# Agent attention followed by a softmax feed-forward layer: p split ahead of its turn, row factors through DRAM, k first in the head, five u buffers, and a new planned order

## The chip, the cores and the metric

The kernel runs on one core of a Trainium2 chip. The metric is the device time of one launch in microseconds (us). Three runs of the kernel before gave a median of 1497.92 us (1496.82 to 1499.42).

## The reference

Four batches, 12608 tokens each, 128 channels, 49 agents, 1024 hidden columns, all in float32:

```python
def sm(a, b):
    s = scale * (a @ b.transpose(0, 2, 1)); s = s - s.max(-1, keepdims=True)
    e = np.exp(s); return e / (e.sum(-1, keepdims=True) + 1e-09)
agent_v = sm(agents, k) @ v
x = sm(q, agents) @ agent_v                      # [50432, 128]
h = x @ w_in                                     # [50432, 1024]
e = np.exp(h - h.max(-1)); solu = h * e / (e.sum(-1) + 1e-09)
ln = (solu - mean) / sqrt(var + 1e-06) * g_ln
out = ln @ w_out
```

## The kernel before, in words

**Tiles and engines.** Tokens are cut into 396 tiles of 128 (99 a batch), and two tiles make a pair. As `agent_v @ w_in` is the same for all tokens of a batch, it is made once a batch (phase A: scores of k, maximum, exponential, transposes, product with v, then `f1` to `f4l`, lines 570 to 590) and kept in two parts, `mh` and `ml`, whose sum is the full value; each has two buffers (`mpool`). Phase B makes the softmax p of 8 tiles of q over the agents: products (line 694), maximum, exponential, sum, then per group of 4 tiles a scaled `pack` on GpSimd (POOL, 722), two transposes on TensorE (PE, 729), a copy to SBUF on ScalarE (ACT, 737), a split into high and low part on POOL (743, 748), and four transfers on SyncE's queue (SP, 767) that place both parts in `pT`, the high one and the low one in different halves of the partitions.

**Each tile x** then goes through `c_h` (824: h in PSUM, four instructions on PE, `pT` against `mh` and `ml`), `c_max` (828, VectorE, DVE), `c_exp` (838, ACT), `c_u` (843, DVE: u = h times e, two buffers of u), and `c_sq` (849, ACT: the sum of squares). Half of the pairs are of kind Z: u is turned on PE (856), copied to SBUF on ACT (907), split into `uH` and `uL` on POOL (916, 920) and multiplied with w_out's two parts in 24 instructions a pair (937). The others are of kind Y: u is turned in 32x32 blocks on DVE (863), regrouped by 16 transfers a unit on SP's queue (871), and multiplied in full float32 (877). Two pairs of one kind make a unit of 4 tiles, with one output transfer (1025).

**The row factor** (one over the standard deviation) is made on POOL in eight small steps (951 to 972). For a Z unit it is turned on DVE (976), sent to DRAM (980), and read back by all partitions as `rB` (984); `c_fin` (1020, DVE) multiplies PSUM by `rB` into `ob`, which is sent out. For a Y unit POOL makes a 128x128 tile `dy` (1002), PE multiplies it with `quad` (1007), and ACT or DVE copies the 128x4 result to `yp` (1011), by which `c_fy` (885 on ACT, 887 on DVE) multiplies.

**The order** is fixed ahead by `Plan.run`: each operation has an engine, a cost, a due time (`D...` constants, in tiles) and what it depends on; the plan always issues next what can start first, and among what can start at about the same time (`EPS`) the one due first. All instructions of an engine then run in that order, and SP's transfers too, each behind the one before it. Transfers are all issued by SP. `WC` = 4 is the number of Z products that are planned as one operation, `YC` = 2 that of Y products (a Y product is two instructions in the profile). Four PSUM banks (`px`) serve everything but h; h has two buffers of two banks. In the head (batch 0), loads of k and v alternate, each product with v following its scores; free times on PE before the first tile are filled with small products (1035).

Of the kernel before, what the change touches and what calls it, by code (L numbers as in the profile page):

```python
# [19 lines left out]
class Op:  # L20


    __slots__ = ("eng", "fn", "cost", "due", "left", "outs", "deps", "take", "free", "bank", "start", "end", "by", "ready", "kind", "shy")


class Plan:
# [8 lines left out]
    SWITCH = ((0.0, 0.0, 0.09), (0.0, 0.0, 0.09), (0.15, 0.12, 0.0))  # L35

    HOLD = 0.12

    def __init__(self, banks):
# [4 lines left out]
        self.kind = 0  # L44

# [14 lines left out]
    def push(self, o):  # L60
        o.ready = {}
        for e in o.eng:
            o.ready[e] = max([0.0] + [d.end + (self.LAT.get(d.by + e, 0.2) if d.by != "S" else 0.0) for d in o.deps])
            self.cand[e].append(o)

    def run(self, idle=None):
        while True:
            best = None
            for e, ops in self.cand.items():
                if not ops:  # L70
                    continue
                free = [b[0] for b in self.banks if b[0] is not None]
                first = min(free) if free else None
                at, opts, low = self.at[e], [], None
                for o in ops:
                    s = max(at, o.ready[e])
                    if o.take:
                        if first is None:
                            continue
                        s = max(s, first)  # L80
                    opts.append((s, o))
                    low = s if low is None else min(low, s)
                if low is None:
                    continue
                near = [z for z in opts if z[0] <= low + self.EPS[e]]
                if e == "P" and self.kind == 2:
                    near = [z for z in opts if z[0] <= low + self.HOLD and z[1].kind == 2] or near
                s, o = min(near, key=lambda z: z[1].due)
                if o.shy > 0.0:
                    s, o = min((z for z in opts if z[0] <= s + o.shy), key=lambda z: z[1].due)  # L90
                if best is None or s < best[0]:
                    best = (s, e, o)
            if best is None:
                break
            s, e, o = best
            for z in o.eng:
                self.cand[z].remove(o)
            if o.take:
# [5 lines left out]
            o.start, o.by = s, e  # L104
            if e == "S":
                hold, size, lag = o.cost
                self.at[e] = s + hold
# [43 lines left out]
def kernel(  # L151
# [25 lines left out]
    CPR = 5.63  # L177
    UTB = 3
# [7 lines left out]
    WC = 4  # L186

    BD0 = 5.03
    BD1 = 15.85
    BD2 = 1.88  # L190
    BD3 = -20.87
    BD4 = -3.24
    BD5 = 3.07
    DH = -9.08
    DMX = 6.59
    DEX = 1.64
    DU_ = -21.8
    DSQ = 15.3
    DT = -0.97
    DEV = 13.79  # L200
    DLD = 12.64
    DSP = 16.84
    DW = 13.2
    DR = 15.79
    DF_ = 37.93
    OUTD = 20.02
    OUTC = -69.6
    VA = 3
    VA1 = 12
    QA = 22.03  # L210
    WA = -7.03
    VLAG = 0.74
    PTB = 4
    SHY = 0.31
    DHR = 5.82
    DHL = -9.02
    DMXR = 19.87
    DMXL = 0.06
    DEXR = -2.43
    DEXL = -3.57  # L220
    DUR = -30.17
    DUL = 17.14
    DSQR = -54.86
    DSQL = 4.96
    DTR = -20.36
    DTL = -14.12
    DEVR = -17.55
    DEVL = 7.51
    DLDR = -20.48
    DLDL = -18.62  # L230
    DSPR = -1.34
    DSPL = -11.65
    DWR = -2.28
    DWL = 3.97
    RBL = 2.38
    ASP = 0.86
    MZ = 5.66
    B7G = True
    B7 = 7.35
    DTB = 4.24  # L240
    DMV = -0.75
    DMS = 0.0
    MVC = 2
    DWY = 11.65
    DWS = 4.05
    YC = 2
    DFY = 5.09
    DTBR = -5.14
    DTBL = -8.26
    ASTART = -4.09  # L250
    AEND = 0.95
# [8 lines left out]
    mpool = ctx.enter_context(tc.tile_pool(name="mpool", bufs=2))  # L260
# [11 lines left out]
    make_identity(nc, ident)  # L272
    ones = const.tile([P, P], F32, name="ones")
# [13 lines left out]
    def pair_f64(dst, names):  # L287
# [5 lines left out]
        def tmp():  # L293
            for k, tg in (("s", "e"), ("a", "e"), ("e", "u"), ("m", "u")):
                t = epool.tile([P, 2, HW], I32, tag=tg, bufs=2, name=f"c{k}_{names}")
                for h in range(2):
                    z[k, h] = t[:, h, :]
# [37 lines left out]
    def load_out():  # L335
        nc.sync.dma_start(out=g_sb, in_=g_ln)
        for h in range(2):
            wd = words["out", h] = mpool.tile([P, HW, 2], I32, tag="mh" if h == 0 else "ml", name=f"wd_out{h}")
# [6 lines left out]
    def conv_out():  # L345
# [8 lines left out]
        def sums(q):  # L354

            n = NF >> (q + 1)
            if q == 0:
                pm["s"] = epool.tile([P, NF // 2, C], F32, tag="sq", bufs=1, name="ws")
# [32 lines left out]
    for i in range(2):  # L391
        pk = const.tile([P, GT, AP2], F32, name=f"pack{i}")
        nc.gpsimd.memset(pk, 0.0)
        packs.append(pk)
# [9 lines left out]
    fold32 = const.tile([P, SQB], F32, name="fold32")  # L404
    nc.vector.tensor_reduce(out=fold32, in_=ident.rearrange("p (a c) -> p c a", c=SQB), op=ALU.add, axis=AX.X)
    quad = const.tile([P, GT], F32, name="quad")
    nc.vector.tensor_reduce(out=quad, in_=ident.rearrange("p (a c) -> p a c", c=SQB), op=ALU.add, axis=AX.X)
    ph2 = [ps_h.tile([P, DF], F32, name=f"ph{i}") for i in range(2)]
    plan = Plan([ps_x.tile([P, HW], F32, name=f"px{i}") for i in range(4)])
    op = plan.op  # L410
# [9 lines left out]
    def phase_a(b, due, gate):  # L420
# [14 lines left out]
        def kload(c):  # L435
            w = CT * P if c < NCK else CKT
            if not head:
                kts[c] = kpool.tile([C, CT * P], F32, tag="kt", name=f"kt{b}_{c}")
            else:
                if c % 4 == 0:  # L440
                    kts["t"] = ypool.tile([C, 4, CT * P], F32, tag="tb", name=f"kh{b}_{c}")
# [3 lines left out]
        def vload(c):  # L445
            if head:
                if c % 4 == 0:
                    vts["t"] = ypool.tile([P, 4, CT, C], F32, tag="uY", name=f"vh{b}_{c}")
# [51 lines left out]
        def p2_et(c, k="D"):  # L500
            px = ps.pop(("t", c))
            w = HW if c < NCK else TX
            eT = res["eT", c] = bpool.tile([P, HW], F32, tag="eT", name=f"eT{b}_{c}")
# [100 lines left out]
        def kop(c):  # L604
            if c < NC and c not in K:
                old = M1.get(c - 1) if not head else M1.get(c - 5 - c % 4)
                K[c] = op("S", st(kload, c), (0.45, sz(c), 0), -199 + 0.2 * c if head else at(c * 2.55 - 3), gate + [old])

        def vop(c):
            old = M2.get(c - 1) if not head else M2.get(c - 5 - c % 4)  # L610
# [4 lines left out]
        FC = {}  # L615
        for c in range(NC):
# [9 lines left out]
            if c:  # L626
                FC[c] = op("A", st(p1_fc, c), 0.2, at(z + 0.6), [N1[c], AC.get(c - 4)])
            TT[c] = op("P", st(p2_t, c), 0.435 * fr(c), at(z + 1), [EE[c], M2.get(c - 2)], take=True)
            ET[c] = (op("A", st(p2_et, c, "A"), 0.478 * fr(c), at(z + 1.2), [TT[c]], free=TT[c]) if head and c < HEADA else
                     op(ETE, st(p2_et, c), (0.478 * fr(c), 0.6 * fr(c)), at(z + 1.2), [TT[c]], free=TT[c]))  # L630
            vop(c)
            M2[c] = op("P", st(p2_mm, c), 0.88 if c < NCK else 0.42, at(z + MZ) if not head else at(z + 1.5),
                       [ET[c], V[c], M2.get(c - 1), AC.get(c - 2)], take=True, kind=2)
            AC[c] = op("D", st(p2_ev, c), 0.26, at(z + 1.8), [M2[c], FC.get(c), AC.get(c - 1)], free=M2[c])
# [46 lines left out]
    def phase_b(k, dues, gate=()):  # L681
# [36 lines left out]

        def b4(q):
            m = min(GT, nt - q * GT)  # L720
            sl = slice(q * GT, q * GT + m)
            nc.gpsimd.tensor_tensor(out=packs[q][:, :m, :A], in0=r["d"][:, sl, :],
                                    in1=r["s"][:, sl].unsqueeze(2).to_broadcast([P, m, A]), op=ALU.mult)

        def b5(q, px):
            m = min(GT, nt - q * GT)
            r["pt", q] = px
            for j in range(0, m, 2):
                nc.tensor.transpose(px[:, j * AP2 : (j + 2) * AP2], packs[q][:, j : j + 2, :].rearrange("p j a -> p (j a)"),
                                    ident)  # L730

        def b6(q):
            w = (min(GT, nt - q * GT) + 1) // 2 * P
            r["n", q] = bpool.tile([P, 2, GT // 2 * P], F32R, tag="pn", bufs=2, name=f"pn{b}_{t0}_{q}")
            if B7G:
                r["f", q] = bpool.tile([P, GT // 2 * P], F32, tag="pf", bufs=2, name=f"pf{b}_{t0}_{q}")
                nc.scalar.copy(out=r["f", q][:, :w], in_=r.pop(("pt", q))[:, :w])
            else:
                nc.scalar.copy(out=r["n", q][:, 0, :w], in_=r["pt", q][:, :w])

        def b7h(q):
            w = (min(GT, nt - q * GT) + 1) // 2 * P
            nc.gpsimd.tensor_scalar(out=r["n", q][:, 0, :w], in0=r["f", q][:, :w], scalar1=1.0, scalar2=0.0, op0=ALU.mult, op1=ALU.add)

        def b7l(q):
            w = (min(GT, nt - q * GT) + 1) // 2 * P
            pn = r["n", q]
# [496 lines left out]
```

## Time and profile before

| | before |
|---|---|
| median of three runs | 1497.92 us |
| profiled execution | 1496.0 us, of which the span 1494.2 us |
| busy PE / DVE / ACT / POOL | 1447.1 / 1371.5 / 1291.3 / 1110.3 us |
| transfers issued on SP's queue, largest groups | uY x768, pT x392 |
| mean granted clock of PE | 0.995 of full |

Busy times are those of instructions on an engine; PE's ends are modelled, and its instructions overlap, so its busy time counts short pauses as work. The chain is the work that ended last, followed back: a piece "1.44 PE px L937 x12" says that twelve instructions of line 937 took 1.44 us of the path. An idle time names what ended it.

### The profile page before, as it was taken

How to read it: one execution, taken by the hardware profiler on the slowest of the kernel's cores; microseconds unless marked ns; L12 is line 12 of the kernel's file. 1: busy time of each engine (PE TensorE's matmuls, PEld its weight loads, DVE VectorE, ACT ScalarE, POOL GpSimd, SP SyncE). 2: the span in 40 equal slices, each digit the busy share in tenths (PEclk: the TensorE clock that was granted, in tenths of full speed). 3: DMA queues.
4: the chain of work that ended last, by engine and by line, in shares of the span. 5: the costliest groups of instructions: out<-in, count | busy, mean ns of one | idle time of the engine just before them, and what ended most of it. 6: DMA issues, size and time to landing. Idle time of an engine off the chain costs nothing.

```text
span 1494.2 us, 34108 instructions
## 1 busy us (share of the span) xinstructions
PE 1447.1 (97%) x11954; PEld 1285.0 (86%) x11954; DVE 1371.5 (92%) x1987; ACT 1291.3 (86%) x2536; POOL 1110.3 (74%) x1569
## 2 busy tenths in 40 slices
PE   8889999999999999999999999899999999999999
PEld 5668889898988989989887888789889898989998
DVE  7799999999999999999998898699999999999996
ACT  4688989889988988899887898688899999999995
POOL 2667787788778777787786677677788888888875
PEclk9999999999999999999999999999999999999999
DMA  9565676676577668756657655567546656566461
GB/s 371 163 179 156 177 186 160 174 184 153 144 194 202 165 179 215 181 137 158 155 140 200 184 156 157 147 175 206 138 118 157 152 126 166 137 154 162 114 155 57
DMA packets 142698, 247.72 MB, mean 166 GB/s; under 512 B 26048, under 2 KB 80320, under 8 KB 142528
## 3 DMA queue, kind: packets, MB, share of 16 engines
q1 hardware_dynamic: 142528, 245.54, 63.1%
q8 instruction: 96, 1.57, 0.5%
q14 instruction: 74, 0.61, 0.1%
HBM read 92.77 MB, written 26.05 MB: 80 GB/s over the span
## 4 chain that ended last, share of the span: by engine, by line
PE 56%; ACT 13%; DVE 10%; DMA 10%; issue 5%; SPq 4%; POOL 2%; DVEq 0%; ACTq 0%; POOLq 0%
PE ph L824 15%; PE px L877 14%; PE px L937 11%; PE px L856 6%; ACT e L838 5%; DVE u L843 4%; DMA rB<-dr 4%; ACT sq L849 4%; DVE nm L828 3%; PE px L465 3%; SPq L871 3%; PE px L514 3%; DMA dr<-yr 2%; ACT uT L907 2%; PE px L694 2%
## 5 line engine op out<-in xcount | busy, mean ns | idle before, releaser
L849 ACT ACTIVATE sq<-u,su 128x1024 bf16<-128x1024 f32 x396 | 460.7, 1163 | 53.4 <-DVE u L843 49.2
L843 DVE SCALAR_TENSOR_TENSOR u<-ph,e 128x1024 f32<-128x1024 f32 x396 | 474.6, 1217 | 29.4 <-ACT e L838 13.6
L838 ACT ACTIVATE e<-ph,nm 128x1024 f32<-128x1024 f32 x396 | 442.8, 1124 | 60.6 <-DVE nm L828 58.9
L828 DVE TENSOR_REDUCE nm<-ph 128x1 f32<-128x1024 f32 x396 | 467.8, 1206 | 28.2 <-PE ph L824 26.8
L920 POOL TENSOR_TENSOR uL<-uT,uH 128x1024 fp32r<-128x1024 f32 (+1 forms) x198 | 470.7, 2377 | 14.5
L877 PE MATMUL px<-w,uY 128*128 128x128 f32 x3072 | 383.0, 276 | 1.7 <-ACT uT L907 1.0
L877 PEld LDWEIGHTS px<-w,uY 128*128 128x128 f32 x3072 | 365.9, 192 | 8.7 <-ACT uT L907 2.3
L824 PE MATMUL ph<-mh,pT 128*128 128x512 f32 x792 | 336.5, 425 | 8.6 <-DVE u L843 5.4
L824 PE MATMUL ph<-ml,pT 128*128 128x512 f32 x792 | 312.8, 395 | 0.0
L916 POOL TENSOR_SCALAR uH<-uT 128x1024 fp32r<-128x1024 f32 (+1 forms) x198 | 207.6, 1048 | 99.2 <-ACT uT L907 99.0
L937 PE MATMUL px<-uH,wH 128*128 128x256 f32 x816 | 238.7, 292 | 0.6 <-POOL x L957 0.3
L863 DVE STREAM_TRANSPOSE tb<-u 128x1024 f32<-128x1024 f32 x192 | 237.2, 1238 | 1.3
L937 PE MATMUL px<-uL,wH 128*128 128x256 f32 x816 | 235.7, 289 | 0.0
L907 ACT COPY uT<-px 128x512 f32<-128x512 f32 x394 | 220.8, 595 | 16.7 <-PE px L856 12.9
L937 PE MATMUL px<-uH,wL 128*128 128x256 f32 x816 | 235.0, 288 | 0.0
L856 PE MATMUL px<-ident,u 128*128 128x128 f32 x1632 | 223.0, 274 | 6.8 <-DVE ob L1020 4.0
L856 PEld LDWEIGHTS px<-ident,u 128*128 128x128 f32 x1632 | 191.2, 141 | 33.4 <-DVE ob L1020 5.1
L824 PEld LDWEIGHTS ph<-mh,pT 128*128 128x128 f32 x792 | 149.8, 189 | 43.7 <-DVE u L843 13.5
L824 PEld LDWEIGHTS ph<-ml,pT 128*128 128x128 f32 x792 | 150.1, 189 | 19.5 <-DVE ml L590 0.3
L937 PEld LDWEIGHTS px<-uH,wL 128*128 128x128 f32 x816 | 153.8, 189 | 5.0 <-issue 2.3
L937 PEld LDWEIGHTS px<-uH,wH 128*128 128x128 f32 x816 | 153.9, 189 | 4.8 <-issue 1.3
L937 PEld LDWEIGHTS px<-uL,wH 128*128 128x128 f32 x816 | 154.1, 189 | 4.2 <-issue 1.1
(132 smaller groups left out, 1595.9 us busy)
## 6 DMA issues: line engine op xcount, KB each, us to landing
uY<-tb SPq DMA_DIRECT2D x768, 128.0 KB, 2.9
pT<-pn SPq DMA_DIRECT2D x392, 64.0 KB, 2.2
qt<-in_qT_dram SPq DMA_DIRECT2D x48, 512.0 KB, 4.4
kt<-in_kT_dram SPq DMA_DIRECT2D x36, 512.0 KB, 4.4
vt<-in_v_dram SPq DMA_DIRECT2D x36, 512.0 KB, 4.8
rB<-dr SPq DMA_DIRECT2D x50, 256.0 KB, 3.7
out_dram<-ob SPq DMA_DIRECT2D x50, 256.0 KB, 2.6
out_dram<-oy SPq DMA_DIRECT2D x48, 256.0 KB, 2.8
```

The source lines that it names most:

```text
L824: nc.tensor.matmul(ph[:, sl], lhs, bmats[b]["mh" if m == 0 else "ml"][:, sl], start=(m == 0), stop=(m == 1))
L828: nc.vector.tensor_reduce(out=nms[x], in_=phs[x], op=ALU.max, axis=AX.X, negate=True)
L838: nc.scalar.activation(out=es[x], in_=phs[x], func=AF.Exp, bias=nms.pop(x), accum_out=st[G]["S"][:, j : j + 1])
L843: nc.vector.scalar_tensor_tensor(out=u, in0=phs[x], scalar=INV, in1=es[x], op0=ALU.mult, op1=ALU.mult, accum_out=su)
L849: nc.scalar.activation(out=sq, in_=u, func=AF.Square, bias=su, scale=-float(DF), accum_out=st[G]["Q"][:, j : j + 1])
L856: nc.tensor.transpose(pt[:, kf * P : (kf + 1) * P], us[x][0][:, k0 * P : (k0 + 1) * P], ident)
L863: nc.vector.transpose(to, us[x][0].rearrange("p (k r c) -> p k r c", r=GT, c=SQB))
L877: nc.tensor.matmul(st[G]["po"][:, a * P : (a + 1) * P], yb[G][1][:, a, kf].rearrange("p x c -> p (x c)"), w2[:, kf, :], start=(kf == 0), s ...
L907: nc.scalar.copy(out=rr[x][:, hf * 4 : hf * 4 + 4, :], in_=pt)
L916: nc.gpsimd.tensor_scalar(out=uH, in0=rr[x][:, k0:k1, :], scalar1=1.0, scalar2=0.0, op0=ALU.mult, op1=ALU.add)
L920: nc.gpsimd.tensor_tensor(out=uL, in0=rr[x][:, k0:k1, :], in1=uH.bitcast(F32), op=ALU.subtract)
L937: nc.tensor.matmul(po, wt[:, kf, :], ut[:, kf, :], start=(q == 0), stop=(q == WM - 1))
```

## The change

- **p is split before it is turned.** POOL scales p in place, rounds it to the high part and subtracts, into a `pack` of 4 x (64 high + 64 low) columns. One transpose a tile in F32R then gives `pT` with both parts in place; ACT copies it from PSUM (128x512) straight into `pT`. The copy to `pf`, the split behind it and the four transfers a group are gone.
- **The Y factor goes through DRAM**, as Z's does: turned on DVE, sent, and read back as 128x4 (`senty`); `y0`, `y1`, `y2` are gone.
- **Head:** all k is asked for first, then v; products with v come behind the whole of the scores, and `eT` of all chunks is kept (in the buffers of `uH`, `uL`). w_in and the first q are asked for behind v.
- **Buffers:** five of u in place of two, `UTB` 4 for 3, `sq` is written over e, `c_fin` writes over `rB` (three buffers), and in return `mh` and `ml` have one buffer: `f4h` waits for the last h of the batch before.
- **Order:** `WC` 12, `YC` 8 (8 products, 16 instructions); tiles' h in order; regrouping, factor and `rB` transfers may be issued by ACT too, but by the plan only where SP is some 30 us late with them, and one behind a long activation; the plan's costs of a change of kind on PE, and all due times, are other numbers.
- The last unit is sent in pieces of 256 bytes (four a partition and half) where it was 1 KB.

```diff
     mpool = ctx.enter_context(tc.tile_pool(name="mpool", bufs=2))
+    mpool = ctx.enter_context(tc.tile_pool(name="mpool", bufs=1))
...
-            o9 = op("A", st(f4h, hf), 0.571, at(z + 0.8 + 0.4 * hf), [o8, l0, last_h.get(b - 2)] + mdone[b])
+            o9 = op("A", st(f4h, hf), 0.571, at(z + 0.8 + 0.4 * hf), [o8, l0, last_h.get(b - 1)] + mdone[b])
...
         def b4(q):
+            nc.gpsimd.tensor_tensor(out=d, in0=d, in1=rs..., op=ALU.mult)
+        def b4h(q):
+            nc.gpsimd.tensor_scalar(out=packs[q][:, :m, 0, :A], in0=d, scalar1=1.0, scalar2=0.0, op0=ALU.mult, op1=ALU.add)
+        def b4l(q):
+            nc.gpsimd.tensor_tensor(out=packs[q][:, :m, 1, :A], in0=d, in1=packs[q][:, :m, 0, :A].bitcast(F32), op=ALU.subtract)
         def b5(q, px):
-            for j in range(0, m, 2):
-                nc.tensor.transpose(px[:, j * AP2 : (j + 2) * AP2], packs[q][:, j : j + 2, :]..., ident)
+            for j in range(m):
+                nc.tensor.transpose(px[:, j * P : (j + 1) * P].bitcast(F32R), packs[q][:, j]..., identR)
         def b6(q):
-            nc.scalar.copy(out=r["f", q][:, :w], in_=r.pop(("pt", q))[:, :w])
+            nc.scalar.copy(out=pt[:, : m * P], in_=r.pop(("pt", q))[:, : m * P])
...
-        us[x] = (epool.tile([P, DF], F32, tag="u", bufs=2, ...), ...)
+        us[x] = (epool.tile([P, DF], F32, tag="u", bufs=UBF, ...), ...)          # UBF = 5
-        sq = epool.tile([P, DF], BF16, tag="sq", bufs=1, name=f"sq{x}")
+        sq = es.pop(x).bitcast(BF16)[:, :DF]
...
-        EX[x] = op("A", F(c_exp, x), 1.11, at(x, DEX, DEXR, DEXL), [MX[x], U.get(x - 2), R2.get(G - SB + 1)] + (cout if x < 2 else []))
+        EX[x] = op("A", F(c_exp, x), 1.11, at(x, DEX, DEXR, DEXL), [MX[x], U.get(x - 2), SQ.get(x - 2), R2.get(G - SB + 1)] + (cout if x < 2 else []))
-        U[x] = op("D", F(c_u, x), 1.21, at(x, DU_, DUR, DUL), [EX[x], T.get((x - 2, 0)), T.get((x - 2, 1)), TBT.get(x - 2), SQ.get(x - 2)])
+        U[x] = op("D", F(c_u, x), 1.21, at(x, DU_, DUR, DUL), [EX[x], T.get((x - UBF, 0)), T.get((x - UBF, 1)), TBT.get(x - UBF), SQ.get(x - UBF)])
...
-                o = op("G", y0, 0.5, x + DR, [o, YP.get(back(G, 2))])
-                p = op("P", y1, 0.3, x + DR, [o], take=True)
-                YP[G] = op("AD", y2, (0.2, 0.08), x + DR, [p, FY.get(back(G, 3))], free=p)
+                TN[G] = op("D", turn, 0.12, x + DR, [o])
+                RB[G] = op("SA", send, (0.5, 0.01, 0), x + DR, [TN[G]])
+                YP[G] = op("SA", senty, (0.5, 0.15, 0), x + DRB, [RB[G], FY.get(back(G, 3))])
...
+        def senty(e):
+            yp = st[G]["yp"] = tiny.tile([P, GT], F32, tag="yp", name=f"yp{G}")
+            port[e].dma_start(out=yp, in_=r["dr"].rearrange("j p -> (j p)").rearrange("(a p) -> p a", p=P))
...
         def c_fin(G, j0=0, j1=GT):
+            rB = obs[G] = st[G]["rB"]
+            z = rB.rearrange("d a j c -> d j a c")[:, j0:j1]
+            nc.vector.tensor_tensor(out=z, in0=st[G]["po", j0 // 2]..., in1=z, op=ALU.mult)
```

## Rows read from the trace of the kernel before

**Rows 1.** The page, busy time of each engine.

```profile
PE 1447.1 (97%) x11954; PEld 1285.0 (86%) x11954; DVE 1371.5 (92%) x1987; ACT 1291.3 (86%) x2536; POOL 1110.3 (74%) x1569
```

**Rows 2.** Busy time by stretch: length, PE, PEld, DVE, ACT, POOL, clock, DMA share, GB/s.

```profile
0.00:20.00 20.00, 14.81 (x91) 7.48 (x91) 11.66 (x29) 7.71 (x17) 5.01 (x17) 1.00 0.91 347
20.00:40.00 20.00, 20.00 (x210) 12.75 (x209) 18.80 (x38) 9.30 (x25) 6.78 (x6) 1.00 1.04 399
60.00:120.00 60.00, 50.74 (x419) 40.72 (x419) 54.66 (x82) 50.94 (x98) 34.38 (x49) 0.97 0.56 149
120.00:1480.00 1360.00, 1331.43 (x10977) 1201.08 (x10976) 1266.33 (x1797) 1206.95 (x2359) 1044.05 (x1471) 1.00 0.64 162
300.00:400.00 100.00, 99.26 (x795) 89.76 (x792) 96.11 (x145) 90.61 (x178) 79.67 (x115) 1.00 0.69 166
700.00:1000.00 300.00, 281.18 (x2306) 249.85 (x2304) 264.46 (x381) 249.35 (x486) 213.07 (x303) 0.98 0.64 168
```

**Rows 3.** The chain that ended last, 395 to 425 us: start, length, what.

```profile
399.95 1.79 PE px L877 x16
...
402.17 0.45 PE px L877 x4
...
407.53 0.47 PE px L937 x4
...
408.44 1.44 PE px L937 x12
...
417.28 0.44 PE px L729 x4
...
419.59 0.12 PE px L1007 x2
```

**Rows 4.** The same chain, 929 to 940 us.

```profile
933.68 0.62 SPq L767
...
935.70 3.22 DMA rB<-dr
938.95 0.70 DVE ob L1020
```

**Rows 5.** Who waited for whom, in total, times, longest.

```profile
DVE ob L1020 <- DMA rB<-dr: 30.2, 18, 8.3
...
SPq L767 <- POOL pn L743: 111.7, 39, 10.6
```

**Rows 6.** DMA issues: count, KB each, median us to landing.

```profile
pT<-pn SPq DMA_DIRECT2D x392, 64.0 KB, 2.2
...
dr<-yr SPq DMA_DIRECT2D x50, 2.0 KB, 2.0
...
out_dram<-ob SPq DMA_DIRECT2D x2, 128.0 KB, 1.7
```

**Rows 7.** Groups by line: busy, mean ns, idle before.

```profile
L907 ACT COPY uT<-px 128x512 f32<-128x512 f32 x394 | 220.8, 595 | 16.7 <-PE px L856 12.9 <-POOL z L963 1.7 <-POOL pack L722 0.6
...
L737 ACT COPY pf<-px 128x256 f32<-128x256 f32 x100 | 38.1, 387 | 7.3 <-PE px L729 7.2
L729 PE MATMUL px<-ident,pack 128*128 128x128 f32 x200 | 37.5, 273 | 2.1 <-DVE ob L1020 2.1
...
L976 DVE STREAM_TRANSPOSE yr<-ycol 128x32 f32<-128x32 f32 x50 | 9.9, 197 | 0.0
...
L590 DVE SCALAR_TENSOR_TENSOR ml<-px,rs,mh 128x512 fp32r<-128x512 f32 x8 | 5.9, 739 | 1.4 <-ACT mh L585 1.4
L585 ACT ACTIVATE mh<-px,rs 128x512 fp32r<-128x512 f32 x8 | 5.5, 694 | 0.7 <-DVE wL L377 0.7
```

**Rows 8.** The chain in the head, 49 to 60 us.

```profile
49.73 0.20 PE px L528
...
54.16 0.49 PE px L570 x2
...
58.07 1.57 PE ph L824 x6
```

More of the change, by code (lines that the diff above doesn't have):

```diff
@@ L20 @@
 class Op:
-    __slots__ = ("eng", "fn", "cost", "due", "left", "outs", "deps", "take", "free", "bank", "start", "end", "by", "ready", "kind", "shy")
+    __slots__ = ("eng", "fn", "cost", "due", "left", "outs", "deps", "take", "free", "bank", "start", "end", "by", "on", "ready", "kind", "shy")
 class Plan:
@@ L44, in __init__ @@
         self.kind = 0
+        self.long = False
+        self.old = set()
     def op(self, eng, fn, cost, due, deps=(), take=False, free=None, after=(), kind=1, shy=0.0):
@@ L63, in push, with pick @@
             o.ready[e] = max([0.0] + [d.end + (self.LAT.get(d.by + e, 0.2) if d.by != "S" else 0.0) for d in o.deps])
+            if e == "A" and o.eng == "SA":
+                o.ready[e] += self.SLACK
             self.cand[e].append(o)
+            self.old.add(e)
+    def pick(self, e):
+        ops = self.cand[e]
+        if not ops:
+            return None
+        first = None
+        if e == "P":
+            free = [b[0] for b in self.banks if b[0] is not None]
+            first = min(free) if free else None
+        at, opts, low = self.at[e], [], 1e9
+        for o in ops:
+            s = o.ready[e]
+            if o.eng == "SA":
+                if e == "A" and not self.long:
+                    continue
+                if s < at:
+                    s = at
+                if e == "S":
+                    s += self.LEAN
+            elif s < at:
+                s = at
+            if o.take:
+                if first is None:
+                    continue
+                if s < first:
+                    s = first
+            opts.append((s, o))
+            if s < low:
+                low = s
+        if not opts:
+            return None
+        top = low + self.EPS[e]
+        near = [z for z in opts if z[0] <= top]
+        if e == "P" and self.kind:
+            near = [z for z in opts if z[0] <= low + (self.HOLD if self.kind == 2 else self.STICK) and z[1].kind == self.kind] or near
+        s, o = min(near, key=self.rank)
+        if o.shy > 0.0:
+            s, o = min((z for z in opts if z[0] <= s + o.shy), key=self.rank)
+        return s, e, o
@@ L66, in run, with rank @@
+    @staticmethod
+    def rank(z):
+        return z[1].due
     def run(self, idle=None):
+        now, self.old = {}, set(self.cand)
         while True:
+            for e in self.old:
+                now[e] = self.pick(e)
+            self.old = set()
             best = None
[L69 to L92, printed above, removed]
@@ L93, in run @@
+            for e in self.cand:
+                if now[e] is not None and (best is None or now[e][0] < best[0]):
+                    best = now[e]
             if best is None:
@@ L95, in run @@
             s, e, o = best
+            if e == "S" and o.eng == "SA":
+                s -= self.LEAN
+            self.old.add(e)
             for z in o.eng:
                 self.cand[z].remove(o)
+                self.old.add(z)
+            if o.take or o.free is not None:
+                self.old.add("P")
             if o.take:
@@ L185 @@
     TD = 2
[L186 to L207, printed above, removed]
+    WC = 12
+    BD0 = 1.1
+    BD1 = 42.63
+    BD2 = 121.82
+    BD3 = -41.9
+    BD4 = 174.88
+    BD5 = -3.51
+    DH = -10.72
+    DMX = 2.05
+    DEX = -501.66
+    DU_ = -82.14
+    DSQ = 174.1
+    DT = -22.79
+    DCP = -46.67
+    DEV = 42.85
+    DLD = 27.07
+    DSP = 45.34
+    DW = 22.53
+    DR = -10.25
+    DF_ = -72.89
+    DRB = -3.56
+    OUTD = -6.59
+    OUTC = -54.84
     VA = 3
     VA1 = 12
-    QA = 22.03
-    WA = -7.03
-    VLAG = 0.74
+    QA = 148.57
+    WA = 253.18
+    VLAG = 123.05
     PTB = 4
[L214 to L251, printed above, removed]
+    SHY = -155.59
+    DHR = -331.25
+    DHL = -106.12
+    DMXR = -3.45
+    DMXL = -26.93
+    DEXR = 135.27
+    DEXL = -209.51
+    DUR = -276.93
+    DUL = 16.41
+    DSQR = -180.79
+    DSQL = -186.0
+    DTR = 42.67
+    DTL = -160.29
+    DEVR = -52.56
+    DEVL = -381.37
+    DLDR = -369.36
+    DLDL = 232.76
+    DSPR = -221.17
+    DSPL = 29.4
+    DWR = 79.47
+    DWL = 0.42
+    RBL = -364.1
+    ASP = 1.09
+    MZ = 2.36
+    DTB = -0.64
+    DMV = -142.87
+    DMS = -208.98
+    MVC = 1
+    DWY = 28.43
+    DWS = 4.7
+    YC = 8
+    DFY = 63.14
+    DTBR = -20.67
+    DTBL = -23.23
+    ASTART = -8.35
+    AEND = -332.2
     engs = (mybir.EngineType.PE, mybir.EngineType.Activation, mybir.EngineType.DVE, mybir.EngineType.Pool)
@@ L272 @@
     make_identity(nc, ident)
+    identR = const.tile([P, P], F32R, name="identR")
+    nc.vector.tensor_copy(out=identR, in_=ident)
     ones = const.tile([P, P], F32, name="ones")
@@ L391 @@
     for i in range(2):
-        pk = const.tile([P, GT, AP2], F32, name=f"pack{i}")
-        nc.gpsimd.memset(pk, 0.0)
+        pk = const.tile([P, GT, 2, AP2], F32R, name=f"pack{i}")
+        nc.gpsimd.memset(pk.bitcast(F32), 0.0)
         packs.append(pk)
@@ L403 @@
     av_dup = const.tile([C, 2 * AP2], F32, name="av_dup")
[L404 to L407, printed above, removed]
     ph2 = [ps_h.tile([P, DF], F32, name=f"ph{i}") for i in range(2)]
     plan = Plan([ps_x.tile([P, HW], F32, name=f"px{i}") for i in range(4)])
+    plan.EPS = {"P": EP, "A": EA, "D": ED, "G": EG, "S": 0.0}
+    plan.HOLD, plan.STICK = HLD, STK
     op = plan.op
@@ L615, in phase_a, with second @@
         FC = {}
+        def second(c):
+            z = c * 2.55
+            vop(c)
+            if c:
+                FC[c] = op("A", st(p1_fc, c), 0.2, at(z + 0.6), [N1[c], AC.get(c - 4)])
+            M2[c] = op("P", st(p2_mm, c), 0.88 if c < NCK else 0.42, at(z + MZ) if not head else at(z + 1.5 + NC),
+                       [ET[c], V[c], M2.get(c - 1), AC.get(c - 2)], take=True, kind=2)
+            AC[c] = op("D", st(p2_ev, c), 0.26, at(z + 1.8), [M2[c], FC.get(c), AC.get(c - 1)], free=M2[c])
+        for c in range(NC if head else 0):
+            kop(c)
         for c in range(NC):
```

227 lines of the change are left out of this document (99 added, 128 removed).

## The prediction

> **What bounds the kernel now.** I read the page's busy times first: PE is busy for 97% of the span, DVE for 92% [rows 1]. A mean like that hides stages, so next came the busy time by stretch. From 120 to 1480 us PE is busy for 1331.4 of 1360 us, DVE for 1266.3 [rows 2]; the reader should see that PE is the fuller engine, with DVE three to four points below, and that PE idles for only 28.6 us there, of which 18.8 lie between 700 and 1000 us, where the mean clock is 0.98 as well. From 300 to 400 us, undisturbed, PE is at 99% and DVE at 96% [rows 2]. The chain that ended last confirms it: from 395 to 425 us it is almost nothing but runs of PE back to back [rows 3]. So work taken from ACT, POOL or SP saves nothing by itself. Three things can save: fewer instructions on PE, fewer pauses of PE, and a shorter head and ramp.
>
> The pauses have a pattern. At 929 to 940 us the chain leaves PE: the last of p's transfers is issued on SP, behind it at 935.7 us the one of rB lands after 3.22 us, and only then DVE's product with rB runs [rows 4]. DVE waits for rB 30.2 us in 18 places, the longest 8.3, and SP itself stands 111.7 us on p's low and high parts from POOL [rows 5]. SP issues in order, so whatever is behind p's transfers is late with them.
>
> **Part by part**, against the profiled execution of 1496.0 us.
>
> *Work on PE.* (1) The Y factor's product goes: 48 units, 0.12 us of the path each [rows 3]: -5.8. (2) p's transposes: 200 in float32 now [rows 7] at 0.44/4 = 0.11 us [rows 3], 22 us in all; afterwards 396 (one a tile) in F32R. No row shows one. The bounds: half of a Z product, which is F32R with 256 columns at 1.44/12 = 0.12 [rows 3], so 0.06; and 0.11, as if F32R brought nothing. As it is the operation of the one and the type of the other, I take the middle, 0.085: 33.7 us, so +11.7 (+1.8 to +21.6). The Trainium skill, in TensorE: Matmul & The Clock Gate, § Back-to-back issue gap, says that in a stream where each product brings its own weights 128 columns come at some 81 ns; by that figure an estimate of this term is +10. No run here shows it yet. (3) Longer runs of products: four Z instructions take 0.47 us of the chain and twelve 1.44, so 0.118 and 0.120 each; four Y instructions 0.45 and sixteen 1.79, 0.113 and 0.112 [rows 3]. A change of kind costs nothing that these rows show. I take 0, and 0 to -3 for the range (0.01 us for each of some 300 runs).
>
> *Pauses of PE.* (4) The four transfers a group leave SP, 392 and a few short ones [rows 6], each 0.62 us of issue [rows 4]: some 240 us of SP's time, with the waits for POOL ahead of them. p's path loses the wait in SP's queue, the issue of several transfers and the 2.2 us to landing [rows 6]; rB is no longer held by it. What is late next is rB's own path: turn, DRAM, back, at 2.0 us [rows 6] and 3.2 us [rows 4], which needs only to come before the last Z product of its unit. (5) Five buffers of u let DVE write u before the transposes, the block turns and the squares of two tiles ago are done. In return exp now waits for the squares of two tiles ago, as they lie in e; both are on ACT, in order, so it costs nothing as long as ACT isn't full. ACT gets 100 x (0.595 - 0.387) = 20.8 us more for the wider copies [rows 7], to about 1310 us: 89% of the new span, covered. What can be had is PE's idle time from 120 to 1480 us (28.6), some 6 us of half clock in 700 to 1000 (2% of 300), and the idle 9.3 us of the ramp from 60 to 120 [rows 2]: 44 us. I take two thirds, -29, since the waits I can name cover most but a static order always meets some wait that it did not plan; the range is 0 to -44.
>
> *DVE.* (6) It gets 48 turns at 0.197 us [rows 7], 9.5 us. Cover: PE's work. Over 120 to 1480 us, shortened by 23, DVE would be at (1266.3 + 9.5)/1337 = 95.4%, within the 96.1% that it reaches at 300 to 400 [rows 2]. If that cover is gone, this costs its 9.5 us; it is the reason why I don't take all 44 us above.
>
> *The Y factor through DRAM.* (7) A transfer out of 2.0 us [rows 6], one back, and the turn stand in place of a product and a copy. The way back, 512 pieces of 4 bytes, is in no row; between dr's 2.0 and rB's 3.2 us it would be ready some 6 us after POOL's last step. It hides behind the unit's 16 regrouping transfers, which at the 0.62 us of an issue [rows 4] take 10 us of SP, and the Y products behind them. Priced at 0; if the cover were gone, a PSUM bank is held for some 3 us longer in 48 units, where three others serve.
>
> *The head.* (8) Both orders ask for the same bytes, some 15.5 MB, and the first 40 us already run at 347 and 399 GB/s [rows 2], so the last load cannot come much ahead of 40 us. What moves is what comes behind it: from the last product with v at 48.7 us the first h takes until 58.1, and from 49.7 to 54.2 PE's path is the maximum over all of k's chunks and its factors [rows 8], which needs no v and is now done before v is in. I take 6 us of that. Bounds: 0, if the conversion of w_in, now asked for behind part of v, holds the first h; -11.6, if the last v is in at 41 us, its product takes 1.3 and f1 to h the 3.9 that they take now [rows 8]: 46.5 us.
>
> *One buffer for mh and ml.* (9) At three batch boundaries f4h must wait for the last h of the old batch. Last h, copy 0.694, difference 0.739 [rows 7], next h: 1.4 us in which PE has Y and Z products to do and DVE the maxima and u of two tiles. I take 1 us each, +3 (0 to +4.3); behind f4h on ACT stand exp and squares, which have slack.
>
> *The tail.* (10) The last unit leaves in pieces of 256 bytes. 128 KB now land in 1.7 us [rows 6]; I take +1. The Trainium skill, DMA: Bandwidth & Descriptors, § Specifications, speaks against it: under 512 bytes a write to memory becomes read and write again; an estimate by that rule is twice the 1.7 us, +1.7. No row has such pieces at the end.
>
> **Sum:** -5.8 + 11.7 + 0 - 29 + 0 - 6 + 3 + 1 = -25.1, so 1471 us against 1496.0. The median of the three runs lies 1.9 us above the profiled execution; I forecast **1473 us** for the median. By the bounds alone it would be from 1438 to 1520. About 0.2% (3 us) can be told from no change here.
>
> **Rivals.** *A, the boundaries drain (slower).* If phase A of the next batch comes to its end late (the plan spreads it wider, `ASP` 1.09 for 0.86, with its last steps due after the batch's first tile), then the last h has gone, f1 to f4l still run one after the other, and the one buffer forbids any h ahead. Then each boundary empties and refills DVE and ACT as the head does: PE's 9.3 us idle of the ramp [rows 2], some 2 us of lower clock (3% of 60) and the 1.4 us of (9), about 12 us, and 36 in all in place of 3: 1506 us. It decides from 8.4 us a boundary on, where 25 + 3 us are used up. For: nothing in the old trace shows a second set of mh and ml idle long ahead. Against: due times only break ties, and a starved DVE takes phase A's steps at once. Chance 0.16.
>
> *B, the order brings nothing.* PE's pauses between 700 and 1000 us came from late answers on this execution's queues, not from p's transfers, and others take their place, so that only 10 us of the 44 are had. With p's transposes at 0.11: -5.8 + 21.6 - 10 - 6 + 3 + 1 = +4, 1502 us; with them at 0.085, -6, 1492. For: the waits in rows 5 say who came last, not why he was late. Against: the chain at 929 us shows the order p, then rB, on SP itself [rows 4]. Chance 0.10.
>
> *C, nearly all pauses go.* -44 and the head's -9, transposes at 0.06: -5.8 + 1.8 - 44 - 9 + 0 + 1 = -56, 1442 us. DVE would then be at 1276/1316 = 97% of the middle, above the 96.1% of the undisturbed stretch [rows 2]; hence 0.12.
>
> The forecast itself, 1452 to 1490, has 0.62. **Chances:** faster 0.62 + 0.12 and a quarter of B, 0.77; within 0.2% half of B, 0.05; slower A and the last quarter of B, 0.18. The range of 8 in 10 runs from 1444, leaving out most of C, to 1502, leaving out most of A.
>
> **What would show it.** Right: no pT on SP's queue; DVE's wait for rB well under 30 us; PE's idle time at 120 to 1480 us under 15; the first h near 52 us; p's transposes at 0.06 to 0.11 us of the chain; runs of w products longer but not cheaper per instruction; DVE near 95%. Wrong: holes in PE and DVE at three places about 360 us apart (A); DVE's waits for yp or for a bank held by a Y unit; ACT filled so that exp waits for squares; PE's pauses where they were (B).

## The result, and the profile after

| | before | after |
|---|---|---|
| median (four runs of each) | 1497.37 us | 1473.36 us (1471.18 to 1474.88) |
| ratio | | 0.9842, 95% interval 0.9817 to 0.9867 |
| span of the profiled execution | 1494.2 us | 1472.0 us |
| first tile's h (head) | 58.07 us | 61.37 us |

The forecast was 1473 us. The first row below is the page's busy line of the kernel after; then its busy time by stretch, with the columns of [rows 2] (length, PE, PEld, DVE, ACT, POOL, clock, DMA share, GB/s).

```profile
PE 1444.8 (98%) x12053; PEld 1277.6 (87%) x12053; DVE 1369.6 (93%) x2019; ACT 1298.1 (88%) x2515; POOL 1069.3 (73%) x1521
```

```profile
0.00:20.00 20.00, 17.39 (x85) 7.92 (x85) 5.95 (x16) 8.66 (x21) 1.97 (x14) 1.00 0.92 351
20.00:40.00 20.00, 18.06 (x174) 11.77 (x172) 16.56 (x37) 12.83 (x33) 7.37 (x10) 0.92 1.04 390
...
60.00:120.00 60.00, 48.52 (x379) 37.06 (x380) 54.05 (x82) 49.03 (x92) 44.00 (x57) 0.94 0.45 125
120.00:1457.00 1337.00, 1332.92 (x11125) 1198.33 (x11124) 1268.87 (x1839) 1220.18 (x2354) 1003.26 (x1432) 1.00 0.56 146
...
700.00:1000.00 300.00, 299.93 (x2524) 266.19 (x2523) 280.88 (x417) 274.27 (x535) 219.74 (x310) 1.00 0.61 162
```

PE's idle time in the middle (from 120 us to 1480 before, to 1457 after) went from 28.6 us [rows 2] to 4.1, and from 700 to 1000 us, where 18.8 us of it and a clock of 0.98 had been, PE is busy throughout at full clock. Head and ramp did not gain: the first 40 us still run at 351 and 390 GB/s, and from 60 to 120 us PE idles 11.5 us where it was 9.3, at a clock of 0.94 for 0.97. Of the waits of the kernel after these stand for DVE (who waited for whom, total, times, longest):

```profile
DVE nm L867 <- PE ph L863: 26.0, 40, 3.0
DVE u L882 <- ACT e L877: 25.8, 60, 1.3
...
DVE rB L1049 <- DMA rB<-dr: 2.8, 1, 2.8
```

The wait for rB of [rows 5] is down from 30.2 us in 18 places to one of 2.8. What DVE still waits for is h and the exponential, in a hundred short pieces. The transfers, as in [rows 6]; pT is gone from them:

```profile
dr<-yr SPq DMA_DIRECT2D x98, 2.0 KB, 1.9
...
yp<-dr SPq DMA_DIRECT2D x48, 2.0 KB, 3.2
...
out_dram<-rB SPq DMA_DIRECT2D x2, 128.0 KB, 2.3
```

All transfers are still issued by SP. The chain from 514 to 530 us shows PE's prices, as in [rows 3]:

```profile
515.10 1.38 PE px L978 x12
516.48 1.84 PE ph L863 x8
518.33 0.64 PE px L808 x8
518.97 1.48 PE px L978 x12
...
520.89 1.79 PE px L918 x16
```

Eight of p's F32R transposes take 0.64 us, 0.08 each. Twelve Z products take 1.38 to 1.48, sixteen Y instructions 1.79, as before.

### The profile page after: what moved, and what is told of

Same layout as the page of the kernel before. It is cut to its first block, busy times and chain, and to the rows that moved or that the text cites. A ratio compares the mean times of both kernels' runs of the same rounds, so it can differ in the third digit from the quotient of the medians.

```text
span 1472.0 us, 33435 instructions
## 1 busy us (share of the span) xinstructions
PE 1444.8 (98%) x12053; PEld 1277.6 (87%) x12053; DVE 1369.6 (93%) x2019; ACT 1298.1 (88%) x2515; POOL 1069.3 (73%) x1521
## 4 chain that ended last, share of the span: by engine, by line
PE 64%; DVE 16%; ACT 12%; issue 4%; DMA 2%; SPq 1%; POOL 1%; ACTq 0%; DVEq 0%; POOLq 0%
PE ph L863 16%; PE px L918 16%; PE px L978 12%; PE px L895 8%; DVE u L882 6%; ACT e L877 5%; DVE nm L867 4%; ACT e L888 3%; ACT uT L948 3%; PE px L519 3%; DVE tb L902 3%; PE px L573 3%; PE px L763 2%; PE px L808 1%; PE px L552 1%
## 5 line engine op out<-in xcount | busy, mean ns | idle before, releaser
L877 ACT ACTIVATE e<-ph,nm 128x1024 f32<-128x1024 f32 x396 | 442.7, 1123 | 84.0 <-DVE nm L867 82.1
L882 DVE SCALAR_TENSOR_TENSOR u<-ph,e 128x1024 f32<-128x1024 f32 x396 | 472.1, 1219 | 28.6 <-ACT e L877 25.8
L961 POOL TENSOR_TENSOR uL<-uT,uH 128x1024 fp32r<-128x1024 f32 (+1 forms) x198 | 470.8, 2378 | 11.7
L888 ACT ACTIVATE e<-u,su 128x1024 bf16<-128x1024 f32 x396 | 459.7, 1165 | 20.9 <-DVE u L882 20.3
L918 PE MATMUL px<-w,uY 128*128 128x128 f32 x3072 | 377.0, 277 | 0.0
L918 PEld LDWEIGHTS px<-w,uY 128*128 128x128 f32 x3072 | 359.6, 192 | 13.3 <-issue 7.8
L978 PE MATMUL px<-uH,wL 128*128 128x256 f32 x816 | 228.6, 280 | 0.0
L978 PE MATMUL px<-uL,wH 128*128 128x256 f32 x816 | 228.3, 280 | 0.2 <-POOL uL L961 0.2
L895 PE MATMUL px<-ident,u 128*128 128x128 f32 x1632 | 217.1, 275 | 2.9 <-DVE uL L953 1.5
L948 ACT COPY uT<-px 128x512 f32<-128x512 f32 x394 | 212.9, 599 | 5.5 <-PE px L895 4.3
L895 PEld LDWEIGHTS px<-ident,u 128*128 128x128 f32 x1632 | 183.9, 141 | 19.6 <-ACT uT L948 2.9
```

Source lines behind the costliest of these rows:

```text
L877: nc.scalar.activation(out=es[x], in_=phs[x], func=AF.Exp, bias=nms.pop(x), accum_out=st[G]["S"][:, j : j + 1])
L882: nc.vector.scalar_tensor_tensor(out=u, in0=phs[x], scalar=INV, in1=es[x], op0=ALU.mult, op1=ALU.mult, accum_out=su)
L888: nc.scalar.activation(out=sq, in_=u, func=AF.Square, bias=su, scale=-float(DF), accum_out=st[G]["Q"][:, j : j + 1])
L895: nc.tensor.transpose(pt[:, kf * P : (kf + 1) * P], us[x][0][:, k0 * P : (k0 + 1) * P], ident)
L918: nc.tensor.matmul(st[G]["po"][:, a * P : (a + 1) * P], yb[G][1][:, a, kf].rearrange("p x c -> p (x c)"), w2[:, kf, :], start=(kf == 0), s ...
L948: nc.scalar.copy(out=rr[x][:, hf * 4 : hf * 4 + 4, :], in_=pt)
```

## The experiments

Each was timed in three rounds beside the kernel before; ratios are to that one, the changed kernel's being 0.9842. The changed kernel itself was not timed again beside them, so a difference to it is good to some 5 us by these intervals. Two kinds stand apart. Some keep the changed kernel's order instruction for instruction on PE, DVE, ACT and POOL, so that only the edit differs. In others an edit makes the plan come out anew; since that alone turned out to move the time by tens of microseconds, most of these had their due times searched again.

**A nudge of the plan.**

```diff
-    DW = 22.53
+    DW = 22.63
```

> The changed kernel with one due time nudged by a tenth of a tile (the Z products, 22.63 for 22.53); all parts as they are, but the plan comes out in another order. If the gain lies in the parts, the time stays within 3 us of 1473. If it lies in this one order, the nudged plan gives part of it back: 1478 to 1490, with PE idle for clearly more than the 4 us that it idles from 120 to 1457 us.

Measured: 1516.98 us, ratio 1.0127 (1.0100 to 1.0154). All parts of the change are in this kernel and it is slower than the one before, by more than I had expected even of the second case. Its middle:

```profile
120.00:1457.00 1337.00, 1301.44 (x10782) 1160.69 (x10781) 1244.48 (x1793) 1176.66 (x2239) 973.76 (x1384) 0.99 0.55 143
```

PE idles 35.6 us there against 4.1; over the whole run DVE waits 51.3 us for h and 17.1 for rB. So the parts alone do not make the time; it needs them and one particular order.

**More work on PE, same order.**

```diff
-  nc.tensor.transpose(px[:, j * P : (j + 1) * P].bitcast(F32R), packs[q][:, j]..., identR)
+  nc.tensor.transpose(px[:, j * P : (j + 1) * P], packs[q][:, j]....bitcast(F32), ident)
```

> The same order, instruction for instruction, with p's transposes in float32 instead of F32R: 396 x (0.11 - 0.075) = 14 us more work on PE. If PE is what bounds the changed kernel, 1485 to 1489. If DVE, which is 95% busy, bounds it, PE's longer runs lie beside DVE's work: 1473 to 1477.

Measured: 1476.39 us, ratio 0.9851 (0.9831 to 0.9871). The chain gives the price:

```profile
517.42 0.87 PE px L808 x8
```

0.109 us each for 0.08, so 396 x 0.029 = 11.5 us of work were added (the 14 of the expectation rested on a rougher 0.075), and the time grew by some 3: a quarter, the value expected if DVE binds. The Trainium skill, TensorE: Matmul & The Clock Gate, § Back-to-back issue gap, had given 81 ns for 128 columns with their own weights; the F32R rows agree with it at 0.08, the float32 rows lie above it at 0.109.

But the head hid a part of the dose. These are the u instructions of the changed kernel and then of this one, one a tile, with the start of the first and the last:

```profile
L882 DVE SCALAR_TENSOR_TENSOR u<-ph,e x396: 1172/1220/1226, 64.6 to 1452.2; 128x1024 f32<-128x1024 f32 x198
L882 DVE SCALAR_TENSOR_TENSOR u<-ph,e x396: 1174/1219/1226, 63.2 to 1455.0; 128x1024 f32<-128x1024 f32 x198
```

Here the first u came 1.4 us earlier, and from 60 to 120 us the clock was 0.97 for 0.94; whether by the edit or by chance isn't shown. From the first u to the last the dose cost 4.2 us; from the seventeenth tile's u on, which starts at 125.6 us in the changed kernel, it cost 5.9: half of it, not a quarter.

**More work on DVE, same order.** To ask the same of DVE, each turn of a row factor was done twice.

```diff
             nc.vector.transpose(r["yr"], r["yt"])
+            nc.vector.transpose(r["yr"], r["yt"])
```

> The changed kernel in its own order, with each of the 98 turns of a row factor on DVE done twice: 98 x 0.197 = 19.3 us more work on DVE, nothing else. If PE bounds the kernel and DVE lies beside it, 1473 to 1477. If DVE is the engine that binds (a dose of 11.5 us on PE cost only 3), 1487 to 1493. If both bind in turn, each takes a share: 1478 to 1484.

Measured: 1486.55 us, ratio 0.9926 (0.9902 to 0.9950), 13.2 us above the changed kernel.

```profile
L1015 DVE STREAM_TRANSPOSE yr<-ycol 128x32 f32<-128x32 f32 x98 | 20.8, 212 | 3.4
...
L1014 DVE STREAM_TRANSPOSE yr<-ycol 128x32 f32<-128x32 f32 x98 | 19.3, 197 | 1.6 <-POOL ycol L1010 1.5
```

The second turns (the first line) take 20.8 us, of which 0.63 comes back as time. The value lies between the two last cases of the expectation. The u instructions again:

```profile
L882 DVE SCALAR_TENSOR_TENSOR u<-ph,e x396: 1173/1219/1226, 64.7 to 1466.6; 128x1024 f32<-128x1024 f32 x198
```

From the seventeenth tile's u on the dose cost 13.4 us, again 0.64 of it, so that the ramp, whose clock was 0.91 for 0.94, has no part in this. By these traces, one execution each, half of what is added to PE comes back, then, and two thirds of what is added to DVE: both bind in turn, though PE has 98% in the page and DVE 93%. Which of them binds more often one dose of each does not settle, as a part of the 13 us may be the factor's path itself, which is 0.2 us longer.

**SP's queue filled again, same order.**

```diff
             nc.scalar.copy(out=pt[:, : m * P], in_=r.pop(("pt", q))[:, : m * P])
+            xx = bpool.tile([P, 2 * P], F32, tag="xx", bufs=2, ...)
+            for i in range(2):
+                w = (m + 1 - i) // 2 * P
+                for r1 in (0, AP2):
+                    nc.sync.dma_start(out=xx[r1 : r1 + AP2, :w], in_=pt[r1 : r1 + AP2, i * w : (i + 1) * w].bitcast(F32))
```

> The same order on all engines; behind each copy of p to SBUF SP issues four transfers of 64 KB again, as before, but into a tile that nobody reads. Theory (SP's queue made rB and the regrouping late): DVE waits for rB again, 10 us and more, and 1480 to 1490. Rival (what cost time was that h itself had to wait for p's transfers, not that SP was full): 1472 to 1475, DVE's wait for rB as after the change.

Measured: 1489.55 us, ratio 0.9935 (0.9913 to 0.9958): the theory's value, 16 us. Of its waits:

```profile
DVE rB L1054 <- DMA rB<-dr: 14.7, 2, 10.2
ACT uT L953 <- PE px L900: 13.0, 6, 9.4
...
PEld px L900 <- DVE rB L1054: 10.9, 6, 9.7
```

rB is late in only two places, but for up to 10.2 us, and DVE, PE and ACT all stand for nearly that long. In the longer one SP issues rB's transfer 10.6 us later than in the changed kernel, whose issues come first:

```profile
406.09 10.82 SPq L912 DMA_DIRECT2D uY<-tb  x16
...
419.38 0.38 SPq L1022 DMA_DIRECT2D rB<-dr  x1
```

```profile
416.98 7.85 SPq L917 DMA_DIRECT2D uY<-tb  x11
...
426.18 1.18 SPq L818 DMA_DIRECT2D xx<-pT  x2
...
429.96 0.45 SPq L1027 DMA_DIRECT2D rB<-dr  x1
```

From 400 us to there SP had issued sixteen of the added transfers (line 818) and waited 5.7 us for ACT's copies of p that they read; the regrouping (uY) and rB's transfer stood behind them in its queue. Transfers that nobody needs hold back one that everybody does. But this order was planned without them; whether a plan that knows of them pays too is the next question.

**p's old path, planned for.** The old `b4` to `b8` with four transfers a group on SP, everything else of the change kept.

```diff
-            d6 = op("G", lambda q=q: b4h(q), ...)
-            B4[k, q] = op("G", lambda q=q: b4l(q), ...)
+            d7 = op("G", lambda q=q: b7h(q), 0.48, dues[5] + 2.5 * q + B7, [a6])
+            d7 = op("G", lambda q=q: b7l(q), 0.7, dues[5] + 2.5 * q + B7 + 0.01, [d7])
+            for i in range(2):
+                pT_op[groups[g]] = op("S", lambda q=q, i=i: b8(q, i), (1.3, 0.13, 0), ...)
```

With it ran three more, all with due times searched again, some 7500 trials each: all parts of the change (from the nudged times) as the control; two buffers of u; and the kernel before planned by the new rules (the new `Plan` with its costs and choices, and longer runs).

```diff
-    UBF = 5              (two u)
+    UBF = 2
...
-    WC = 4               (the kernel before, by the new rules)
+    WC = 12
-    YC = 2
+    YC = 8
```

> The control of this group: the changed kernel with all its parts, from the nudged due times, which were then searched again (some 7500 random changes of due times, each kept or dropped by where the plan itself says that it ends). If the order is what the nudge spoiled, a search wins much of it back: 1480 to 1492, against 1517 nudged and 1473 as given. If the nudge cost time in another way, 1505 or more.

> p turned first and split behind it, with its four transfers a group on SP, as before the change; all other parts of the change kept, five u included; due times searched again with as many trials as in the control. Theory (SP's in-order queue holds rB and the regrouping back behind p): 10 to 20 us above the control, DVE waiting for rB 10 us and more. Rival: within 5 us of the control.

> Two buffers of u in place of five, due times searched again with as many trials as in the control. Theory (the buffers decouple DVE from the transposes and squares): 10 to 25 us above the control. Rival (only the order counts): within 5 us of the control.

> The kernel before with all its parts, but planned by the new rules (costs of a change of kind, choice among operations, longer runs), due times searched as in the control. If the gain is the new planning, 1470 to 1485. If it is the parts, 1495 or more: the plan can be no better than two buffers of u and 1400 transfers on SP allow.

| due times searched anew | median us | ratio (95%) | DVE's wait for rB |
|---|---|---|---|
| all parts (control) | 1497.76 | 0.9999 (0.9980 to 1.0018) | 14.9 us in 8 places |
| p's old path | 1479.62 | 0.9879 (0.9859 to 0.9899) | none |
| two u | 1561.90 | 1.0441 (1.0423 to 1.0458) | 82.1 us in 34 places |
| parts of before, new rules | 1584.30 | 1.0581 (1.0562 to 1.0600) | 82.5 us in 33 places |

The transfers of the kernel with p's old path:

```profile
pT<-pn SPq DMA_DIRECT2D x392, 64.0 KB, 2.8
...
rB<-dr SPq DMA_DIRECT2D x50, 256.0 KB, 4.1
```

It has all 392 of p's transfers back on SP, and DVE doesn't wait for rB at all; it is 6 us slower than the changed kernel and 18 faster than the control, where theory and rival had it above the control or level. My theory is refuted as to the gain: in a plan that counts them, p's transfers on SP need not make rB late. The control lies between its own two cases: its search won back 19 of the nudge's 44 us. That search moved no due time by more than 33, the one with p's old path moved some by over 200; if p's old path gains nothing by itself, the 18 us say how far two searches of equal length can lie apart, so nothing smaller is to be read from this table. Two u, though, cost 64 us over the control, the theory's direction at well over its 10 to 25, and the new rules on the old parts gave the slowest kernel of all, far into the second case. In both DVE waits 82 us for rB, and with two u PE's transposes of u (line 895) then wait for DVE's product with rB:

```profile
DVE rB L1049 <- DMA rB<-dr: 82.1, 34, 7.1
...
PE px L895 <- DVE rB L1049: 44.4, 15, 6.3
```

The first line below is the middle of the kernel with two u, the second that of the one with p's old path.

```profile
120.00:1457.00 1337.00, 1278.09 (x10562) 1134.34 (x10562) 1207.49 (x1744) 1152.17 (x2206) 958.06 (x1355) 0.99 0.54 141
```

```profile
120.00:1457.00 1337.00, 1318.28 (x10880) 1174.98 (x10879) 1269.77 (x1844) 1188.98 (x2292) 1022.33 (x1431) 1.00 0.64 164
```

With two u PE, DVE and ACT all do 40 us and more less in the same stretch than in the control (1318.5, 1258.7 and 1199.3 there): it is not one engine that is full, they all wait. With p's old path DVE is as busy as in the changed kernel.

**Five u alone, in the kernel before.** Old rules of planning, old p path and Y factor; only the buffers change. Beside it, as its control, the kernel before with all its parts, nudged and searched alike.

```diff
-    DW = 13.2
+    DW = 13.3            (the control alone)
+    UBF = 5              (from here on, the other alone)
-        us[x] = (epool.tile([P, DF], F32, tag="u", bufs=2, ...), ...)
+        us[x] = (epool.tile([P, DF], F32, tag="u", bufs=UBF, ...), ...)
-        sq = epool.tile([P, DF], BF16, tag="sq", bufs=1, name=f"sq{x}")
+        sq = es.pop(x).bitcast(BF16)[:, :DF]
-    mpool = ctx.enter_context(tc.tile_pool(name="mpool", bufs=2))
+    mpool = ctx.enter_context(tc.tile_pool(name="mpool", bufs=1))
```

> One part alone: the kernel before, with its old rules of planning, its p path and its Y factor, and only the buffers changed: five of u, sq written over e, and in return one of mh and ml; due times searched again, some 5700 trials. Theory, after the last group (the u buffers take up what comes late, rB above all, so that DVE and PE go on): 1470 to 1488, DVE's wait for rB under 12 us. Rival (the other parts and rules are needed too): 1495 or more, DVE waiting for rB some 30 us as before.

> The control for the run beside it: the kernel before with all its parts, two buffers of u included, from due times nudged by a tenth of a tile (Z products, 13.3 for 13.2) and searched again with as many trials. If an order of the old kernel stands and falls with its search as the new one's does, 1500 to 1525; if the old kernel is robust, 1495 to 1500.

Measured: five u 1496.96 us, ratio 0.9990 (0.9976 to 1.0004); the control 1513.54, ratio 1.0104 (1.0077 to 1.0132). Against the kernel as given five u alone bring nothing, which is the rival's value; against its control, planned with the same effort, they bring 16.6 us, less than the 18 that two searches lay apart. That the old order stands and falls with its search as well was the first case of the control's expectation. DVE's wait for rB, five u first:

```profile
DVE ob L1021 <- DMA rB<-dr: 24.8, 12, 4.5
```

```profile
DVE ob L1020 <- DMA rB<-dr: 36.2, 19, 9.2
```

It is a third lower, not below 12 us as the theory had it; orders with the same parts differ by more (2.8 us after the change, 17.1 after the nudge), so that five u shorten it isn't shown. What the two groups together show is that the worth of five u hangs on the rules: with two u the old rules gave 1497 and 1514 us, the new ones 1562 and 1584; with five the old rules gave 1497, the new ones, in six orders, 1473 to 1517.

**The head.**

```diff
-    WA = 253.18
+    WA = -7.03
```

> The changed kernel with w_in asked for first, ahead of k (a new plan follows). Theory (the first h is late, at 61.4 us, because w_out's conversion, which follows w_in's, stands in DVE's queue ahead of phase A's end): both conversions move into the first 30 us, where DVE is idle for most of the time, and the first h comes at 54 to 58 us; 1467 to 1471 if the rest of the plan is as good. Rival (the head is bound by the loads of k and v): first h at 60 us or later, as 1 MB more stands ahead of k; 1473 or more.

Measured: 1500.54 us, ratio 1.0007 (0.9991 to 1.0023). The head did what the theory said; its first h in the chain:

```profile
57.86 0.55 PE ph L863 x2
```

3.5 us ahead of the changed kernel's 61.37. But the plan behind it came out anew, and lost 27 us and more (PE busy for 1315.4 of the 1340 us from 120 to 1460). The head's theory holds as to the head; as a better kernel it failed.

**A try at a better order.**

```diff
-    SWITCH = ((0.0, 0.08, 0.17, 0.08, 0.08), (0.0, 0.0, 0.09, 0.02, 0.0), (0.15, 0.12, 0.0, 0.15, 0.12), ...
+    SWITCH = ((0.0, 0.03, 0.05, 0.03, 0.03), (0.0, 0.0, 0.05, 0.02, 0.0), (0.1, 0.1, 0.0, 0.1, 0.1), ...
```

> A try at a better order: the changed kernel, with the plan's costs of a change of kind on PE cut to 0 to 0.05 us (0.1 for leaving phase A's products), since the traces show next to none, and the due times searched from the given ones, some 14000 trials. If truer costs make a better order, 1464 to 1471. If the larger costs are a margin that the order needs, 1475 to 1490.

Measured: 1478.53 us, ratio 0.9870 (0.9844 to 0.9896). Close to the changed kernel, not below it, and in the second case; as searches lie 18 us apart, that the larger costs are a margin is not shown by it. Its first h comes at 62.59 us. No version that I ran beats the changed kernel.

## Why the prediction was right, and where it was wrong

The time was right to half a microsecond; the reasoning behind it was not, in three places, and that errors of both signs cancelled is luck.

**What bounds the kernel.** I argued from busy time that PE bounds it and DVE is beside it. In the changed kernel the doses say that both bind in turn: of what was added on DVE two thirds came back, of what was added on PE half, behind the ramp. PE's busy time includes its short pauses, as its ends are modelled; DVE's 95% (1268.9 of 1337) leave it little. Whether it was so before the change as well was not tried.

**The pauses, (4) and (5).** Their size was right: -29 forecast, and PE's idle time in the middle fell by 24.5 us, and of 10.2 us there at half clock 3.4 are left. The cause that I put first, SP's queue with p's transfers ahead of rB, fell: a plan that knows of these transfers has no wait for rB at all. Which part took the pauses away instead stays open. What the runs show is that the new rules need the five buffers of u: 64 us between the kernels with five and two in the new parts, more than the 44 between the fastest and the slowest order with five. In the old parts it was 16.6 us against a searched order and nothing against the one given, which is within the spread of searches. How five u help is only argued: an instruction on DVE that comes when its transfer is late holds everything behind it, and the more tiles of u may lie open, the later the plan can set it.

**The head, (8).** I took -6 us, the first h near 52; it was +3.3, at 61.4. Two steps failed. One is where the last product with v ends: at 52.1 us, where it was 48.8 before; what held it back isn't shown. The other is that k's part, done earlier, would shorten what follows: from that product to the first h it is 9.3 us in both kernels. The chain before the first h shows what stood there in its place:

```profile
52.11 3.59 DMA vt<-in_v_dram
55.70 1.58 POOL w L364
57.28 0.02 issue
57.30 1.51 DVE w L364
58.81 0.48 DVE logits L775
59.29 0.66 DVE ml L649
59.95 0.52 DVE sm L783
...
60.69 0.63 DVE ml L649
...
61.37 0.51 PE ph L863
```

DVE's queue has the conversion of w_out (line 364) ahead of `ml`, and that waits for POOL. (The chain puts POOL's own wait down to a load of the next batch's v, landed at 55.7 us; DVE's last conversion step ahead of it ended at 55.55 and may as well have been it.) I had named w_in's conversion as the bound on that side, and not seen that DVE, idle for 14 of the first 20 us, would do both conversions after that. Asking for w_in first left the last product with v at 52.0 and brought the first h to 57.86: what follows v is then 5.9 us, so 3.4 us of the shortening are there, and the later v takes about as much.

**The smaller terms.** p's transposes came to 0.08 us where I took 0.085, so +9.7 in place of +11.7; the Y product is gone; longer runs are no cheaper, as (3) said; DVE's share is 94.9%, forecast 95.4; no wait for yp shows, whose way back lands in 3.2 us (7). The single mh and ml cost next to nothing: around the three boundaries, from 395 to 415, 760 to 780 and 1115 to 1135 us, where the copies into mh run, PE is busy for 59.8 of 60 us, where (9) had 1 us each and rival A twelve. In the tail the last 128 KB land in 2.3 us for 1.7, +0.6 where (10) had 1. The Trainium skill, DMA: Bandwidth & Descriptors, § Specifications, would by the prediction's estimate have made that +1.7; the row shows a third of it.

What (10) left out is that more stands behind the last u. Before, its instructions ran so:

```profile
L843 DVE SCALAR_TENSOR_TENSOR u<-ph,e x396: 1181/1220/1228, 62.2 to 1479.2; 128x1024 f32<-128x1024 f32 x198
```

From the last u's start to the end of the span it was 15.0 us, after the change 19.8; 3.0 of the difference is work that the new order leaves for PE there (14.5 us for 11.5).

The profiled span fell by 22.2 us where the sum had -25.1. From the first u to the last the kernel gained 29.4 us (1417.0 to 1387.6), where the work on PE, the pauses and the boundaries sum to -20.1: 9 better. The head, by the first u, and the end lost 2.4 and 4.8 us, where the sum has -5 for both: 12 worse. That these nearly cancel is luck. Three slips in the prediction's sums change nothing here: rival A decides from 9.4 us a boundary on (28 over three), not 8.4; the head's bound is 46.2 us, not 46.5; and the lower end by the bounds alone is 1435 with (3)'s -3, not 1438. The forecast's chance of 0.62 was too high for another reason: it did not see that the order by itself moves the time by more than the whole forecast. With all parts in, five orders gave 1473, 1479, 1498, 1501 and 1517 us.

**What stays open.** How much of the 24 us belongs to the parts and how much to a luckier or longer search. Like against like, all parts searched lie 15.8 us below the old parts searched (1497.76 against 1513.54), given against given 24.0, and five u alone give the whole of the first difference; but two searches of the same length were 18 us apart. The Y factor, the longer runs and mh's second buffer were not tried alone, as a new plan would have hidden them.

## What to carry to other kernels

Where the order is planned by a greedy rule, any edit is also a new order: keep the order fixed and change one thing in it, or search both sides alike, before a part gets the credit. To find which engine binds, give each a dose of some ten microseconds in the same order and see what comes back; the shares of busy time (98 and 93%) did not show here that both engines give back half and more. What buffers on the tile that links the engines are worth depends on the order around them: three more of u made 64 us under the new rules, and nothing clear under the old.

## What I had not expected of the hardware

A changed due time of a tenth of a tile cost 43.6 us (1516.98 against 1473.36), 31 of it as more idle time of PE in the middle. And transfers whose data nobody reads, 400 of 64 KB or less on SP's queue, cost 16 us: DVE waited 14.7 us for two late transfers, where it had waited 2.8 for one, and the longer of the two stopped three engines for some 10 us.
